# Dealing the weight conversion, the MLP work and two turnings of a fused HGRN2 + MLP kernel anew

## The chip, the cores and the metric

The kernel runs on one core of one Trainium2 chip. The metric is the device time of one launch in microseconds (us). The core has five engines that run side by side, each its own list of instructions in order, and wait for one another by semaphores: TensorE (PE) for matmuls, with its weight loads shown as PEld, VectorE (DVE), ScalarE (ACT), GpSimd (POOL), and SyncE (SP), which here only starts DMA transfers.

## The reference

```python
def _attn_ref(q, k, v, f_logit):          # each (4, 8, 768, 48)
    f = 1.0 / (1.0 + np.exp(-f_logit))
    state = np.zeros((B, H, D, D))
    for t in range(S):
        state = f[:, :, t, :, None] * state + np.einsum('bhd,bhe->bhde', k[:, :, t], v[:, :, t])
        y[:, :, t] = np.einsum('bhd,bhde->bhe', q[:, :, t], state)
    return y

x = attn_out.transpose(0, 2, 1, 3).reshape(B * S, H * D)      # 3072 tokens x 384
h = x @ w_in                                                  # 384 x 2048
g = h * (1.0 / (1.0 + np.exp(-1.702 * h)))
out = g @ w_out                                               # 2048 x 384
```

A gated linear recurrence over 768 steps in four batches of eight heads makes the tokens; an MLP with a quick GELU follows.

## The kernel before, in words

**Units.** The 3072 tokens are cut into 12 units of 256 tokens, three for each batch, numbered 0 to 11. For each unit the recurrence is computed in chunks of 64 tokens: `turn` (L325) brings f, q and k with tokens along the columns (for units 0 to 2 by matmuls, L339, from unit 3 on by a DVE transpose, L327); six levels of products within a chunk follow, each a set of score matmuls (L384), a masked evacuation from PSUM on DVE (L410, tile A), a product of A with v (L448, into y) and a promotion of q and k by the gates of that level (L436, L437 or L439 on DVE, with copies Kc and Qc on ACT, L423). `turn_k` (L498) transposes the keys for the states (matmul L505, copy kn L506); L523 multiplies them with v, L538 to L543 carry the states from chunk to chunk on DVE, and L563 adds the states' part to y. At last y goes through ACT (yT, L571) and six DMA transfers (L592, L597) into xT, the 384 x 256 input of the MLP.

**Parts.** `parts_of(n)` (L814) lists what a unit does as parts, each with a letter: W or V for a level or two levels, T for half of the key transposes, S for the states, B and K for beginning the next unit. Beginning the next unit means `begin_f` (turn f, apply the sigmoid, start the load of the f after next), `begin` (turn q, two small POOL copies of its last column, start the next load of q), `begin_k` and `begin_gates`. From unit 3 on the f and q of the next unit are begun together in one part of letter B.

**MLP work.** The MLP of finished units waits in a list `fill`, in items of a weight in columns: an item of the first product (tile h, three matmuls of 256 columns, L727, followed by the sigmoid on ACT, L732, and the product g on DVE, L733) weighs 768, one of the second (o, L755) 384. From unit 3's tokens on the second product is done with seven half-size products instead of eight (L704), from sums of weights (T, L622) and of g (L641 to L650). `merge` (L848) writes out a unit's parts and deals `columns` of this list between them: after each part comes a portion according to `share` of its letter (W 3, V 4, S 3, T, B and K 1). An item is only taken if the weights that it needs are ready.

**Weights.** The weights come as 64-bit floats, and the kernel itself makes 32-bit floats of them. They are 32 pieces of 128 x 384. A pair of pieces is fetched by one or two DMA transfers into a tile `bits`, of which there are three (L180), and each piece is then converted by one copy on ACT (L208) and five operations on DVE (L223, L219, L226, L227, L228). `convert` (L231) issues one of these DVE operations; `merge` deals 5 x `pieces` of them over its unit, before all MLP items that follow them. A pair that is done starts the fetch of another. Unit 0 has conversion work, but no MLP work yet.

**Order.** PE's order is that in which the program writes its instructions. The other engines follow the written order up to the end of unit 3 (`fill_order`, L90 and L907); behind it the framework's scheduler places their instructions. The last number of `merge`, `by`, is the part of the unit by which its conversion is to be done.

Of the kernel before, what the change touches and what calls it, by code (L numbers as in the profile page):

```python
# [23 lines left out]
def kernel(  # L24
# [34 lines left out]
    B, H, S, D = q.shape  # L59
    DM = H * D  # L60
# [16 lines left out]
    N_FILL = 3  # L77
# [153 lines left out]
    def convert():  # L231

        if state["begin"] < len(pairs) and len(todo) <= NOP:
            begin_pair(state["begin"])
            state["begin"] += 1
        if todo and todo[0]:
            todo.pop(0)()
        if todo and todo[0] is None:
            todo.pop(0)
            state["done"] += 2  # L240
            fetch_weights()
# [34 lines left out]
    def load_vl(n, l):  # L276

        if n >= NALL:
            return
        t = vls[n, l] = ld.tile([P, DM], F32, tag=f"vl{l}", name=f"vl_{n}_{l}")  # L280
        if n < N_TURN:
            pt = ps.tile([P, DM], F32, tag="mm", name=f"tv_{n}_{l}", bufs=4)
            for g in range(NG):
                nc.tensor.matmul(
                    pt[g * 64:(g + 1) * 64], lhsT=perm[:, l - 1, :] if l else ident[:, ::2], rhs=vns[n][:, g, :],
                    start=True, stop=True,
                )
            nc.scalar.copy(t, pt)
            return
        nc.sync.dma_start(out=t, in_=v_toks[n % 2].rearrange("(n two m) e -> two n m e", two=2, m=LEV[l])[0])  # L290
# [507 lines left out]
    def mlp_blocks(*blocks):  # L798

        hs, os = zip(*(mlp_block(n, r) for n, r in blocks))  # L800
        return sum(hs, []) + sum(os, [])


    def keep_up(times):

        if times:
            pt = ps.tile([P, NL * 64], F32, tag="mm", name=f"idle_{next(serial)}", bufs=4)
        for _ in range(times):
            nc.tensor.matmul(pt, lhsT=ident, rhs=masks.rearrange("p l t -> p (l t)"), start=True, stop=True)

    units = [attention(n) for n in range(NALL)]
    LAG = 18 * DM

    def parts_of(n):  # L814

        parts = list(units[n][1])
        _, inter = parts.pop()
        if n:
            kind, scores = parts[0]
            _, ahead = units[n - 1][1][-1]  # L820
            parts[0] = kind, lambda: (ahead(), scores())
        if n < N_TURN:

            def with_v(l):
                kind, fn = parts[l]
                return kind, lambda: (fn(), load_vl(n, l) if n == 0 or l else None, keep_up(2 * (n == 0 and l < 3)))
            parts[:NL] = [with_v(l) for l in range(NL)]
        if n + 1 < NALL:
            begin_f, begin, begin_k, begin_gates = units[n + 1][0]
            i = len(parts)  # L830
            if n + 1 < N_FILL:

                parts.append(("K", lambda: (begin_k(), begin_gates(), load_vl(n + 1, 0) if n + 1 < N_TURN else None)))
                parts.insert(i - 4, ("B", begin if n == 0 else lambda: None))
                parts.insert(i - 5, ("B", begin_f))
                if n:

                    kind, head = parts[0]
                    parts[0] = kind, lambda: (head(), begin())
            else:  # L840
                kind, states = parts.pop()
                parts += [("B", begin_k), (kind, lambda: (states(), begin_gates()))]
                parts.insert(i - 3, ("B", lambda: (begin_f(), begin())))
        else:
            parts.append(("W", inter))
        return parts

    def merge(n, fill, columns, share, pieces=0, hold=0, by=1.0, chores=()):  # L848

        parts = parts_of(n)
        total = sum(share(kind) for kind, _ in parts)
        converting = {"W": 3, "T": 3, "B": 1} if n < N_FILL - 1 else {"W": 3, "V": 4, "S": 3, "T": 1, "B": 1}
        total_ops = sum(converting.get(kind, 0) for kind, _ in parts)
        held = sum(share(kind) for kind, _ in parts[:hold])
        at = at_ops = done = ops = 0
        for kind, fn in parts:
            ready = state["done"]
            fn()  # L860
            for chore in chores[:2]:
                chore()
            chores = chores[2:]
            at += share(kind)
            at_ops += converting.get(kind, 0)
            n_ops = min(int(pieces * NOP * at_ops / (by * total_ops)), pieces * NOP) - ops
            ops += n_ops
            first, n_columns = done, max(0, columns * (at - held) / (total - held) - done)

            def some(end):  # L870
                nonlocal done
                while fill and done < end and fill[0][2] <= ready:
                    w, emit, _ = fill.pop(0)
                    emit()
                    done += w
            for i in range(n_ops):
                some(first + n_columns * i / n_ops)
                convert()
            some(first + n_columns)
# [4 lines left out]
    UNIT = NFF * NK * U + U // P * NFF * DM  # L884
# [12 lines left out]
        load_raw(1, j)  # L897
    load_vn(1)
    fill = []
    merge(0, fill, 0, steady, 8)  # L900
    fill += mlp_blocks((0, 0)) + mlp_blocks((0, 1))
    merge(1, fill, UNIT // 2 - LAG // 2, steady, 10, hold=1)
    fill += mlp_blocks((1, 0), (1, 1)) + mlp_blocks((0, 2), (1, 2))
    merge(2, fill, UNIT, steady, 8)
    fill += mlp_blocks((2, 0), (2, 1)) + mlp_blocks((2, 2), (0, 3)) + mlp_blocks((1, 3), (2, 3))
    merge(3, fill, 3 * UNIT // 2 - LAG // 2, steady, 6, by=0.7)
    fill_order.close()  # L907
    for n in range(3, NALL):
        fill += mlp_unit(n)
# [33 lines left out]
```

## Time and profile before

| | us |
|---|---|
| median of four runs | 657.4 (655.48 to 658.79) |
| the profiled execution | 657.54 |
| its span, first to last instruction | 655.5 |
| PE busy | 634.5 (97% of the span) |
| DVE busy | 444.9 (68%) |
| ACT busy | 229.8 (35%) |
| POOL busy | 54.7 (8%) |

The busy time of PE is the time in which at least one matmul is under way. Units 0 to 11 follow each other in the span: unit 0 ends at about 44 us, unit 1 at 86, unit 2 at 143, unit 3 at 211, and from there each takes some 49 us, up to the MLP of the last unit at the end. [...]

### The profile page before, as it was taken

What the parts mean: (1) busy time and instruction counts of PE and PEld (TensorE: products, weight loads), DVE (VectorE), ACT (ScalarE), POOL (GpSimd) and SP (SyncE); (2) the same over time, 40 slices, a digit from 0 to 9 for tenths busy, and PEclk for the clock granted to TensorE, in tenths of its full rate; (3) what the DMA queues carried; (4) which work ended last, traced back from release to release, by engine and by line L of the source; (5) the groups of instructions that cost most, each with busy time, mean ns of one, the idle gap of its engine ahead of it and who ended that gap; (6) DMA issues with size and microseconds to landing.
All of it is one profiled execution on the core that took longest, in us unless ns stands there. A gap on an engine that the chain in (4) does not pass through costs nothing.

```text
span 655.5 us, 20397 instructions
## 1 busy us (share of the span) xinstructions
PE 634.5 (97%) x8958; PEld 543.2 (83%) x8958; DVE 444.9 (68%) x802; ACT 229.8 (35%) x477; POOL 54.7 (8%) x116
## 2 busy tenths in 40 slices
PE   6969989999999999999999999999999999999997
PEld 5656667666678689989989989989989889989997
DVE  2997978788887657658658558558558557553571
ACT  4473443233224324324324324324324334222120
POOL 3020020020001002002002002002002002000000
PEclk9997999999999999999999999999999999999999
DMA  8887875394135544524514515605604202101000
GB/s 190 217 210 192 203 172 134 93 216 79 34 72 141 147 94 119 149 46 119 155 37 121 155 37 120 165 27 124 162 27 105 66 25 62 39 2 26 25 1 24
DMA packets 67554, 67.67 MB, mean 103 GB/s; under 512 B 30410, under 2 KB 61290, under 8 KB 67466
## 3 DMA queue, kind: packets, MB, share of 16 engines
q1 hardware_dynamic: 67466, 66.38, 40.5%
q8 instruction: 70, 1.15, 0.8%
q14 instruction: 18, 0.15, 0.1%
HBM read 56.92 MB, written 8.65 MB: 100 GB/s over the span
## 4 chain that ended last, share of the span: by engine, by line
PE 85%; DVE 8%; SPq 2%; DMA 2%; ACT 1%; issue 1%; DVEq 0%; ACTq 0%
PE h L727 37%; PE o_X L704 7%; PE o L755 7%; PE o_Y L704 7%; PE o_Z L704 7%; PE sc L384 5%; PE y L448 5%; PE o_W L704 4%; PE y L563 2%; PE sc L523 1%; PE tkn L505 1%; DMA bits<-in_moe_w_in_dram 1%; DVE X L439 1%; SPq L251 1%; DVE s L219 1%
## 5 line engine op out<-in xcount | busy, mean ns | idle before, releaser
L727 PE MATMUL h<-xT,w_in 128*128 128x256 f32 (+1 forms) x1152 | 261.7, 383 | 4.4 <-DMA xT<-yT 1.8
L727 PEld LDWEIGHTS h<-xT,w_in 128*128 128x128 f32 x1152 | 216.7, 191 | 38.9 <-issue 3.1
L733 DVE TENSOR_TENSOR g<-h,sg 128x256 f32<-128x256 f32 (+1 forms) x192 | 80.9, 423 | 100.4 <-ACT sg L732 98.0
L732 ACT ACTIVATE sg<-h 128x256 f32<-128x256 f32 (+1 forms) x192 | 73.4, 384 | 194.5 <-PE h L727 189.7
L423 ACT COPY Kc<-X 128x512 f32<-128x512 f32 x69 | 46.2, 669 | 118.1 <-DVE X L439 84.7
L755 PE MATMUL o<-w_out,g 128*128 128x384 f32 x192 | 66.1, 493 | 0.0
L439 DVE TENSOR_TENSOR X<-X,tot 128x1024 f32<-128x1024 f32 x45 | 55.1, 1225 | 15.3 <-PE sc L384 10.2
L755 PEld LDWEIGHTS o<-w_out,g 128*128 128x128 f32 x192 | 35.3, 190 | 22.9 <-issue 1.4
L704 PE MATMUL o_X<-w_out,g 128*128 128x192 f32 x288 | 51.9, 329 | 0.0
L704 PE MATMUL o_Y<-T,S 128*128 128x192 f32 x288 | 51.1, 331 | 0.1
L704 PEld LDWEIGHTS o_Y<-T,S 128*128 128x128 f32 x288 | 46.5, 190 | 2.6 <-DVE u L679 1.2
L704 PEld LDWEIGHTS o_X<-w_out,g 128*128 128x128 f32 x288 | 47.3, 190 | 0.9
L410 DVE TENSOR_TENSOR A<-sc,masks 128x512 f32<-128x512 f32 x72 | 46.8, 680 | 0.0
L448 PE MATMUL y<-A,vl 64*48 64x64 f32 x2304 | 41.6, 218 | 1.5 <-issue 1.4
L376 POOL TENSOR_TENSOR tot<-F 128x512 f32<-128x512 f32 x12 | 12.5, 1042 | 350.3 <-DVE st L540 350.3
L448 PEld LDWEIGHTS y<-A,vl 64*48 64x48 f32 x2304 | 36.5, 121 | 5.0 <-issue 4.7
L327 DVE STREAM_TRANSPOSE X<-raw 128x1024 f32<-128x1024 f32 x18 | 36.7, 2037 | 2.4 <-PE y L563 2.0
L571 ACT COPY yT<-y 48x512 f32<-48x512 f32 x48 | 27.9, 580 | 12.5 <-PE y L563 12.0
L384 PEld LDWEIGHTS sc<-X,Kc 48*64 48x64 f32 x1344 | 23.9, 134 | 8.3 <-issue 3.5
L384 PE MATMUL sc<-X,Kc 48*64 48x64 f32 x1344 | 28.1, 219 | 1.9 <-DVE A L410 1.2
L376 POOL TENSOR_TENSOR tot<-tot 128x256 f32<-128x256 f32 (+4 forms) x60 | 27.4, 458 | 4.7
L704 PE MATMUL o_Z<-w_out,g 128*128 128x192 f32 x144 | 26.6, 331 | 0.0
(93 smaller groups left out, 656.9 us busy)
## 6 DMA issues: line engine op xcount, KB each, us to landing
vl<-v_tok SPq DMA_DIRECT2D x60, 192.0 KB, 2.8
bits<-in_moe_w_out_dram SPq DMA_DIRECT2D x8, 768.0 KB, 10.2
bits<-in_moe_w_in_dram SPq DMA_DIRECT2D x8, 576.0 KB, 7.1
v_tok<-in_v_dram SPq DMA_DIRECT2D x10, 384.0 KB, 4.4
vn<-v_tok SPq DMA_DIRECT2D x10, 384.0 KB, 6.8
xT<-yT SPq DMA_DIRECT2D x24, 144.0 KB, 2.8
raw<-in_q_dram SPq DMA_DIRECT2D x18, 192.0 KB, 4.2
raw<-in_f_logit_dram SPq DMA_DIRECT2D x18, 192.0 KB, 4.9
```

The costliest lines, as they stand in the source:

```text
L327: nc.vector.transpose(out.rearrange("p (a i j) -> p a j i", a=NP, j=R), raw[:, j].rearrange("p a (j d) -> p (a j) d", j=R)[:, :, :32],)
L376: nc.gpsimd.tensor_tensor(tn, t2[:, :, 0], t2[:, :, 1], ALU.mult)
L384: nc.tensor.matmul(out[g * HS:(g + 1) * HS, h, a, :], lhsT=lhs(h, a * U + g * G), rhs=rhs(h, a * U + g * G), start=True, stop=True,)
L410: nc.vector.tensor_tensor(A[:, :, c:c + w].rearrange("p h (x t) -> p h x t", t=64), t["sc"][:, :, c:c + w].rearrange("p h (x t) -> p h x t ...
L423: nc.scalar.copy(c.rearrange("p (n m) -> p n m", m=m), X[:, j, :NA].rearrange("p (n two m) -> p n two m", two=2, m=m)[:, :, hf, :],)
L439: nc.vector.tensor_tensor(qk, qk, by, ALU.mult)
L448: nc.tensor.matmul(dst(h, g, a), lhsT=vls[n, u][g * 64:(g + 1) * 64, (2 * a + h) * D:(2 * a + h + 1) * D], rhs=A(h, g, a), start=(start an ...
L704: nc.tensor.matmul(t[bank], lhsT=lhs(f), rhs=rhs(f), start=(new and f == 0), stop=(f == HF - 1), skip_group_check=True,)
L727: nc.tensor.matmul(ph, lhsT=w_in[:, c, ff * P:(ff + 1) * P], rhs=xTs[n][:, c, :], start=(c == 0), stop=(c == NK - 1))
L732: nc.scalar.activation(sg, ph, AF.Sigmoid, scale=1.702)
L733: nc.vector.tensor_tensor(g[ff // FG][:, ff % FG, :], ph, sg, ALU.mult)
L755: nc.tensor.matmul(t["po"], lhsT=g[ff // FG][:, ff % FG, tt * P:(tt + 1) * P], rhs=w_out[:, ff, :], start=(ff == ffs[0]), stop=(ff == ffs[ ...
```

## The change

Three things change, all in how work is dealt.

1. The 32 weight pieces are dealt over units 0 to 3 as 6, 10, 9 and 7 instead of 8, 10, 8 and 6.
2. By the end of unit 1, 3 x 384 = 1152 columns less of MLP work have been issued, and in unit 2 1152 more, so that from the end of unit 2 on the amount done is as before.
3. When the next unit is unit 5 or a later one (in `parts_of` n is above 3), f and q are begun in two parts instead of one: f behind the third pair of levels, as before, and q one part later, behind the first half of the key transposes. The unit so has one more part of letter B, and the shares of its parts add up to 20 instead of 19.

```diff
             else:
                 kind, states = parts.pop()
                 parts += [("B", begin_k), (kind, lambda: (states(), begin_gates()))]
-                parts.insert(i - 3, ("B", lambda: (begin_f(), begin())))
+                if n > N_FILL:
+                    parts.insert(i - 3, ("B", begin_f))
+                    parts.insert(i - 1, ("B", begin))
+                else:
+                    parts.insert(i - 3, ("B", lambda: (begin_f(), begin())))
...
     fill = []
-    merge(0, fill, 0, steady, 8)
+    merge(0, fill, 0, steady, 6)
     fill += mlp_blocks((0, 0)) + mlp_blocks((0, 1))
-    merge(1, fill, UNIT // 2 - LAG // 2, steady, 10, hold=1)
+    merge(1, fill, UNIT // 2 - LAG // 2 - 3 * DM, steady, 10, hold=1)
     fill += mlp_blocks((1, 0), (1, 1)) + mlp_blocks((0, 2), (1, 2))
-    merge(2, fill, UNIT, steady, 8)
+    merge(2, fill, UNIT + 3 * DM, steady, 9)
     fill += mlp_blocks((2, 0), (2, 1)) + mlp_blocks((2, 2), (0, 3)) + mlp_blocks((1, 3), (2, 3))
-    merge(3, fill, 3 * UNIT // 2 - LAG // 2, steady, 6, by=0.7)
+    merge(3, fill, 3 * UNIT // 2 - LAG // 2, steady, 7, by=0.7)
```

## The prediction

> **What bounds the kernel now.** I read the page first, then busy time by stretch, then the timeline inside the stretches that were not full. On the page TensorE (PE) is busy 97% of the span, so only the remaining 21 us, and stretches whose clock is low, can be won without removing matmuls. The stretches show where they lie (columns: stretch; its length; busy us and instruction count of PE, weight loads, VectorE = DVE, ScalarE = ACT, GpSimd; granted PE clock; DMA share; GB/s):
>
> ```profile
> 14.00:44.00 30.00, 25.48 (x623) 17.45 (x622) 29.72 (x67) 14.70 (x28) 1.54 (x6) 1.00 0.86 212
> 44.00:57.00 13.00, 10.68 (x148) 7.83 (x152) 8.03 (x18) 6.74 (x12) 4.19 (x8) 0.74 0.81 194
> 57.00:86.00 29.00, 29.00 (x560) 20.74 (x561) 28.02 (x68) 14.14 (x30) 0.42 (x1) 1.00 0.83 219
> 86.00:95.00 9.00, 7.25 (x113) 4.66 (x114) 7.79 (x15) 4.64 (x8) 3.21 (x6) 1.00 0.65 135
> 95.00:127.00 32.00, 32.00 (x366) 24.34 (x367) 22.20 (x50) 9.31 (x21) 0.00 (x0) 1.00 0.46 117
> 127.00:160.00 33.00, 29.33 (x346) 20.73 (x347) 29.39 (x52) 13.18 (x27) 3.76 (x8) 1.00 0.66 147
> 160.00:258.00 98.00, 98.00 (x1241) 77.70 (x1234) 70.83 (x119) 31.03 (x66) 7.00 (x13) 1.00 0.38 98
> 258.00:566.00 308.00, 307.92 (x4695) 283.09 (x4695) 204.67 (x325) 110.02 (x227) 29.41 (x52) 1.00 0.37 94
> ```
>
> Unit 0 (14 to 44 us) has no MLP work to fill PE, and DVE is full there: 29.72 of 30.00. In unit 1 (57 to 86) both engines are nearly full. From 160 us on PE has no gap: what DVE does there is hidden, up to the idle time that it has. The end of unit 0, where PE waits for DVE and ACT, in the timeline (start, duration, engine, line; in brackets the idle time before and its releaser):
>
> ```profile
> 34.08 0.68 DVE L436 TENSOR_TENSOR X<-X,tot 128x512 f32<-128x512 f32 x1
> 34.91 1.07 PE L505 MATMUL tkn<-ident,X 128*128 128x128 f32 x8 [1.07 <-DVE X L436]
> 37.21 1.00 ACT L208 ACTIVATE a<-bits 128x384 f32<-128x384 f32 x2 [0.91 <-DMA bits<-in_moe_w_in_dram]
> 38.11 0.56 ACT L506 COPY kn<-tkn 128x512 f32<-128x512 f32 x1
> 38.73 0.68 PE L523 MATMUL sc<-vn,kn 64*64 64x48 f32 x32 [1.50 <-ACT kn L506]
> 40.31 1.02 DVE L219 SCALAR_TENSOR_TENSOR s<-bits,a 128x384 int32<-128x384 int32 x2
> 41.25 0.35 DVE L538 COPY st<-sc 128x192 f32<-128x192 f32 x1
> ```
>
> **Part 1: two pieces fewer in unit 0.** Two pieces are ten DVE operations. In pairs the rows read 0.62 (L223), 1.02 (L219), 0.62 (L226), 1.02 (L227), 1.02 us (L228): 4.30 us. Not all of it is on the path. The first level scores start at 21.07, 24.43, 28.04 and 31.90, and between them PE is full (gaps of 0.72 and 0.17 only, and the first of them waits for ACT, which waits for weight bits), so DVE running ahead wins 0.17 there at most. The gain lies after 31.9. I walk the new order with the old durations. L436 of the last level, now behind four pending conversion operations instead of six, can start when its score ends, at about 32.7 instead of 34.08; the key transposes (L505) follow at 33.7, not 34.91. In the new ACT order the two L208 copies stand before the first key copy, and none is left between the two key copies: they end at 36.1 and 36.7 (before: 36.29 and 38.67). The second half of L523 ends at about 37.4, not 39.4. The DVE chain from the last evacuation to the first state copy (L538) holds 11 conversion operations instead of 14: from 34.6 on, 0.5 + 0.62 + 1.02 + 1.02 + 0.62 + 1.02 = 4.8 us, so L538 at 39.4 against 41.25. **-1.85 us.** The bounds are the PE gaps that could go at most (4.5 us in the stretch) and no gain at all, if the arrival of weight bits (ACT waited 1.50 and 0.91 us for them) holds the new order too.
>
> **Part 2: 1152 columns fewer by the end of unit 1.** In the new order that is two hidden tiles (h_0_6, h_0_7), each six matmul records. Twenty-four such records take 5.42 us in the row at 94.87, two tiles 2.6 us with overlap. Do they shorten unit 1? Only if PE sets its end. The states (L540) start at 82.67, though their matmuls (L523) ended at 80.07: DVE was still converting. Ten pieces are converted in unit 1 in both kernels, and only one product g (0.42 us) leaves the queue ahead of the states. **-0.4**; PE then idles some 2.6 us before the last y. That work goes into the hand-over to unit 2:
>
> ```profile
> 86.61 5.43 PE L755 MATMUL o<-w_out,g 128*128 128x384 f32 x16
> 94.87 5.42 PE L727 MATMUL h<-xT,w_in 128*128 128x256 f32 x24 [1.75 <-DMA xT<-yT]
> ```
>
> From the end of y (86.0) to that h are 8.9 us, the way of y through ACT and DMA into xT. PE has 7.1 us of work for them; with 2.6 more it has 9.7. The wait of 1.75 goes, and 0.8 us is now PE's own. **+0.8**, so the move by itself returns about 0.4 and wins nothing: the 2.6 us that it takes from unit 1 were hidden behind DVE.
>
> **Part 3: one piece more in unit 2, one more in unit 3.** Each is five DVE operations, 2.15 us, with one L208 copy of 0.5 us on ACT and its share of a weight fetch on the SP queue. Cover: from 95 to 127 DVE idles 9.8 us, from 160 to 258 27 us, while PE has no gap. The fetches come later by a pair; their stretches have a DMA share of 0.46 and 0.38. Without cover the two would cost 4.3. The open place is 127 to 160, where DVE works 29.39 of 33 and PE loses 3.67:
>
> ```profile
> 126.85 2.05 DVE L327 STREAM_TRANSPOSE F<-raw 128x1024 f32<-128x1024 f32 x1
> 128.74 2.02 DVE L327 STREAM_TRANSPOSE X<-raw 128x1024 f32<-128x1024 f32 x1
> 130.85 2.86 PE L727 MATMUL h<-xT,w_in 128*128 128x256 f32 x12 [1.33 <-ACT kn L506]
> 153.33 2.96 PE L727 MATMUL h<-xT,w_in 128*128 128x256 f32 x12 [0.85 <-DVE sum L793]
> ```
>
> In the new order the two turnings stand one g earlier, so that g waits behind them, its PSUM buffer comes free later, and the stall at 130.85 can grow by some 0.9. Against that, between the turnings and the first g of unit 2's MLP stand 18 conversion operations instead of 16 (+0.95) but neither of the two L622 subtractions (-1.82). I take **0**, from -1.5 to +2.
>
> **Part 4: f and q apart.** This concerns the turnings of units 5 to 11. DVE is not in written order there, the scheduler places it, and the listing of both kernels has the same DVE order in these units: F, one or two L650, then q, as in the trace:
>
> ```profile
> 305.82 2.05 DVE L327 STREAM_TRANSPOSE F<-raw 128x1024 f32<-128x1024 f32 x1 [0.83 <-DMA vl<-v_tok]
> 307.71 1.29 DVE L650 TENSOR_TENSOR g<-g,S 128x512 f32<-128x512 f32 x2
> 309.38 2.06 DVE L327 STREAM_TRANSPOSE X<-raw 128x1024 f32<-128x1024 f32 x1 [0.38 <-PE y L563]
> ```
>
> They are apart already: q must wait for the y of the unit before. With q go its two POOL copies (0.65 and 0.41 us) and four loads of raw q on the SP queue; in the listing these trade places with two output stores and two vl loads, and raw q is turned a unit, 48 us, later. What does change is the spread: one more part of share 1 makes 20 shares of 19, so a V part gets 4608 of the 23040 columns instead of 4851, 0.4 us of PE less before the next score. The next score's keys are ready at 315.86, PE reaches it at 318.86: slack 3 us. PE is busy 307.92 of 308.00. **0**; from -2 (o_Y groups at 2.87 instead of 2.60) to +1.
>
> **The clock, rule against row.** From 49 to 56 us the granted clock was half, after PE had been busy 0.77, 0.47, 0.30 and 0.30 in four slices of a microsecond:
>
> ```profile
> 48.00:49.00 1.00, 0.30 (x18) 0.15 (x10) 1.00 (x3) 1.00 (x3) 0.45 (x2) 1.00 0.15 30
> 49.00:50.00 1.00, 0.30 (x13) 0.30 (x16) 1.00 (x3) 0.28 (x2) 0.40 (x1) 0.64 0.20 57
> 50.00:51.00 1.00, 1.00 (x31) 0.86 (x25) 1.00 (x2) 0.71 (x1) 0.00 (x0) 0.50 0.62 134
> ```
>
> The longest single gap there was 1.40 us, and the first twelve h records took 4.76 us instead of some 2.7: 2.1 us. The Trainium skill ("TensorE: Matmul & The Clock Gate", on HAM oscillation) asks for gaps under about 3.4 us, and adds that the window runs free of the kernel. By the gap rule the 2.6 us of new idle time in unit 1 cost nothing; by the row a thin stretch is enough, and a drop there would cost as much as here: 7 us at half clock, 3.4 us of work. The measurement decides that it can happen. For the likeliest case I leave the old drop where it is and add none; the range holds both.
>
> **Sum.** -1.85 - 0.4 + 0.8 + 0 + 0 = -1.45 us on the profiled execution, 657.54 (span 655.5 and 2.0 around it): 656.1. Its time is 0.1 above the median of 657.4, so I forecast 655.9: -0.2%, a small gain, inside what a measurement of this kernel can tell (0.5%, 3.3 us; the four runs spread over 3.3).
>
> **Rivals.** *The relief is larger:* with DVE ahead, PE is denser around 46 to 50 us and the clock drop goes (-2.1), and the stalls of 0.85 and 0.51 us near 155 close with the L622 moved back (-1.4): 655.9 - 3.5 = 652.4. For it: DVE is full in unit 0. Against: the chain y, ACT, xT around 46 us is the same in both kernels. *A new clock drop makes it slower:* unit 1 leaves PE idle 2.6 us before the last y at about 82; if that halves the clock for 7 us, the hand-over, now full of PE work, pays all 3.4 us: 659.3; with the stall at 130.85 grown as bounded, 661. It decides from a drop of about 3 us on, which loses the 1.5 won. *The turnings matter:* if a score's chain were late by 0.4 us once a unit, seven units would cost 2.8: 658.7; the slack of 3 us speaks against. *Nothing happens:* weight bits hold unit 0 as before: 657.8.
>
> **How the numbers follow.** Likeliest case 0.45 (own range 654.3 to 657), larger relief 0.25, clock drop 0.15, turnings 0.05, nothing 0.10. Over 0.5% faster needs under 654.1: most of the relief case and a little of the first, 0.30. Over 0.5% slower needs over 660.7: part of the drop case and mis-sized edges, 0.12. Same 0.58. The range leaves out one in ten on each side: 652 to 660.5.
>
> **What would show it.** After: L538 of unit 0 near 39.4; no wait for xT in front of the first h of unit 1's tokens, which starts near 93.4; PE idle between 75 and 83; PE full from 160 us on, and units 48.5 to 48.8 us apart. Wrong would be: a gap in front of a score after 258 us, a half clock elsewhere, or a stall of more than 3 us between 125 and 160.

## The result

The changed kernel takes 654.07 us (median of 38 runs, 651.58 to 661.53) against 657.78 (57 runs, 655.42 to 661.44) for the kernel before on the same chip: ratio 0.9953, 95% interval 0.9942 to 0.9965. It was measured a second time beside other variants (experiment 10): 655.4 against 657.13, ratio 0.9970 (0.9945 to 0.9996). The ratios are taken from the fast runs alone (one of the 38, at 661.53, was slow) and are not the quotient of the medians, which is 0.9944. The forecast was 655.9, with -0.2%; measured was, by the two ratios, -0.3% and -0.5%. The profiled execution took 654.37 us, its span is 652.2 (before: 655.5), PE is busy for 632.5 us of it.

Busy time by stretch of the changed kernel (stretch; its length; busy us and instruction count of PE, weight loads, DVE, ACT, POOL; granted PE clock; DMA share; GB/s):

```profile
14.00:44.00 30.00, 27.29 (x692) 19.07 (x683) 27.64 (x61) 16.06 (x31) 4.57 (x9) 1.00 0.92 218
44.00:57.00 13.00, 11.09 (x177) 7.46 (x175) 10.14 (x22) 7.16 (x14) 2.24 (x6) 0.87 0.75 160
57.00:86.00 29.00, 27.79 (x517) 20.07 (x518) 27.88 (x66) 15.67 (x33) 3.63 (x6) 1.00 0.91 234
86.00:95.00 9.00, 9.00 (x94) 6.12 (x93) 6.75 (x15) 2.08 (x5) 0.00 (x0) 1.00 0.49 94
95.00:127.00 32.00, 30.23 (x361) 22.56 (x359) 25.60 (x51) 10.56 (x24) 0.41 (x2) 1.00 0.44 117
127.00:160.00 33.00, 29.57 (x440) 22.04 (x441) 28.04 (x53) 12.05 (x26) 3.40 (x7) 1.00 0.72 167
258.00:566.00 308.00, 308.00 (x4590) 284.45 (x4583) 203.53 (x325) 109.39 (x229) 28.02 (x48) 1.00 0.37 94
```

DVE is no longer full in unit 0 (27.64 of 30, was 29.72), PE is fuller there (27.29, was 25.48), the granted clock in the second row is 0.87 (was 0.74), and the hand-over to unit 2 (86 to 95) has no gap. PE loses 1.21 us in unit 1 (57 to 86), where it lost nothing before. The 1.77 us that it loses from 95 to 127 belong to a stall that stood in the next row before; the two rows together lose 5.20, and lost 3.67.

The end of unit 0 in the timeline (start, duration, engine, line; in brackets the idle time before and its releaser):

```profile
32.68 0.69 DVE L436 TENSOR_TENSOR X<-X,tot 128x512 f32<-128x512 f32 x1
32.73 0.69 PE L384 MATMUL sc<-X,Kc 48*64 48x64 f32 x32
34.60 1.10 PE L505 MATMUL tkn<-ident,X 128*128 128x128 f32 x8
34.70 0.55 DVE L219 SCALAR_TENSOR_TENSOR s<-bits,a 128x384 int32<-128x384 int32 x1
36.66 1.17 PE L523 MATMUL sc<-vn,kn 64*64 64x48 f32 x64 [0.38 <-ACT kn L506]
39.05 0.35 DVE L538 COPY st<-sc 128x192 f32<-128x192 f32 x1
```

L538 comes at 39.05 (was 41.25), although this execution began late: its third score stands at 22.14 (was 21.07; this differs from run to run). From the third score to L538 are 16.91 us, where there were 20.18: unit 0 is 3.3 us shorter.

The hand-over to unit 2 and the boundary from unit 2 to unit 3 in the timeline of the changed kernel:

```profile
85.28 3.39 PE L755 MATMUL o<-w_out,g 128*128 128x384 f32 x10
89.68 2.20 PE L755 MATMUL o<-w_out,g 128*128 128x384 f32 x6
91.87 3.48 PE L727 MATMUL h<-xT,w_in 128*128 128x256 f32 x15
...
122.56 2.05 DVE L327 STREAM_TRANSPOSE F<-raw 128x1024 f32<-128x1024 f32 x1
124.44 2.03 DVE L327 STREAM_TRANSPOSE X<-raw 128x1024 f32<-128x1024 f32 x1
127.43 4.15 PE L727 MATMUL h<-xT,w_in 128*128 128x256 f32 x18 [2.21 <-ACT kn L506]
150.90 5.45 PE L727 MATMUL h<-xT,w_in 128*128 128x256 f32 x24 [1.67 <-DVE sum L793]
```

The wait of 1.75 us for xT is gone. The stall for kn has grown from 1.33 to 2.21 us, and one of 1.67 for the sum L793 stands where 0.85 (for L793) and 0.51 (for a g) stood. Why PE waits longer for kn, the copy of the transposed keys, stands in ACT's order. Before:

```profile
130.22 0.58 ACT L506 COPY kn<-tkn 128x512 f32<-128x512 f32 x1
131.42 1.06 ACT L208 ACTIVATE a<-bits 128x384 f32<-128x384 f32 x2
```

After:

```profile
125.66 0.98 ACT L208 ACTIVATE a<-bits 128x384 f32<-128x384 f32 x2
126.80 0.57 ACT L506 COPY kn<-tkn 128x512 f32<-128x512 f32 x1
```

With the new deal of pieces two conversion copies (0.98 us) stand on ACT ahead of the first key copy. From the third score on, with the time lost to half clock taken out (3.4 us before, 1.7 after), the difference splits so:

| from, to | before | after | difference |
|---|---|---|---|
| third score to L538 (unit 0) | 20.18 | 16.91 | -3.3 |
| to the first score of unit 2 (unit 1) | 41.3 | 41.2 | -0.1 |
| to the first score of unit 3 (unit 2) | 57.2 | 58.8 | +1.6 |
| to the end | 512.3 | 511.4 | -0.9 |
| sum | 631.0 | 628.4 | -2.7 (rounded) |

Read the single rows with care: experiments 3 and 4 below, one program in effect, differ by 1.0 us in the row of unit 1 and by 1.6 in the last, but by 0.2 in the sum. The 1.6 us of unit 2 are mostly work: PE has twelve h matmuls more to do there and two o matmuls fewer, 2.0 us by the rates of the rows shown (5.42 us for 24 and 5.43 for 16), and stands still for 3.4 us instead of 3.7.

The rest of the 3.3 us between the two spans is no merit of the change: 1.7 us less half clock, against 1.1 us of later start.

The last row holds a gain in the later units, which are now 48.5 us apart (were 48.5 to 48.8; the first distance, 48.4, is the same in both). Two stretches of timeline show it. Before, in unit 7:

```profile
361.42 2.76 PE L704 MATMUL o_Z<-T,g 128*128 128x192 f32 x16
362.68 1.24 DVE L439 TENSOR_TENSOR X<-X,tot 128x1024 f32<-128x1024 f32 x1 [0.17 <-ACT Qc L423]
363.82 0.35 DVE L679 TENSOR_TENSOR u<-p,o_Y 128x192 f32<-128x192 f32 x1
364.22 2.57 PEld L704 LDWEIGHTS o_Y<-T,S 128*128 128x128 f32 x16 [0.33 <-DVE u L679]
364.22 2.87 PE L704 MATMUL o_Y<-T,S 128*128 128x192 f32 x16
```

After, in the same unit:

```profile
359.04 2.76 PE L704 MATMUL o_Z<-T,g 128*128 128x192 f32 x16
360.74 0.35 DVE L679 TENSOR_TENSOR u<-p,o_Y 128x192 f32<-128x192 f32 x1
361.64 1.46 PE L704 MATMUL o_Y<-T,S 128*128 128x192 f32 x8
363.03 0.69 PE L384 MATMUL sc<-Qc,Kc 48*64 48x64 f32 x32
365.02 1.24 PE L704 MATMUL o_Y<-T,S 128*128 128x192 f32 x6
```

The second o_Y group goes on in the PSUM tile that L679 reads, so it can't start before L679 is through. Before, L679 stood on DVE behind the promotion L439 of the score just done, and PE lost 0.33 us. After, L679 is done 0.5 us ahead of the group, and the score cuts the group in two. In the list of waits of the weight loads from 258 to 566 us the kernel before has 1.2 us of this in four waits, the changed kernel none.

### The profile page after: what moved, and what is told of

The parts are those of the page before. It is cut to its first block, busy times and chain, and to the rows that moved or that the text cites. A ratio compares the mean times of both kernels' runs of the same rounds, so it can differ in the third digit from the quotient of the medians.

```text
span 652.2 us, 20388 instructions
## 1 busy us (share of the span) xinstructions
PE 632.5 (97%) x8958; PEld 543.6 (83%) x8958; DVE 445.0 (68%) x802; ACT 229.2 (35%) x477; POOL 55.0 (8%) x116
## 3 DMA queue, kind: packets, MB, share of 16 engines
q8 instruction: 70, 1.15, 0.8%
## 4 chain that ended last, share of the span: by engine, by line
PE 86%; DVE 6%; DMA 3%; SPq 2%; ACT 1%; issue 1%; DVEq 0%; ACTq 0%
PE h L727 37%; PE o_X L704 8%; PE o_Y L704 7%; PE o L755 7%; PE o_Z L704 7%; PE sc L384 5%; PE y L448 5%; PE o_W L704 4%; DMA bits<-in_moe_w_in_dram 2%; PE y L563 2%; PE sc L523 1%; PE tkn L505 1%; DVE s L219 1%; SPq L180 1%; SPq L251 1%
## 5 line engine op out<-in xcount | busy, mean ns | idle before, releaser
L439 DVE TENSOR_TENSOR X<-X,tot 128x1024 f32<-128x1024 f32 x45 | 55.2, 1227 | 33.9 <-PE sc L384 29.1
L704 PE MATMUL o_X<-w_out,g 128*128 128x192 f32 x288 | 53.8, 331 | 0.0
L704 PE MATMUL o_Z<-T,g 128*128 128x192 f32 x144 | 24.9, 326 | 0.0
(93 smaller groups left out, 660.5 us busy)
```

The lines of the kernel that those rows point to most:

```text
L439: nc.vector.tensor_tensor(qk, qk, by, ALU.mult)
L704: nc.tensor.matmul(t[bank], lhsT=lhs(f), rhs=rhs(f), start=(new and f == 0), stop=(f == HF - 1), skip_group_check=True,)
```

## The experiments

Each was run in five rounds beside the kernel before: 1 to 4 on one chip, 5 to 8 on a second, 9 to 11 on a third, 12 on a fourth. Times are best compared on one chip; from chip to chip go by the ratios. "Rest" in the table is the span less the start of the third score and less the time lost to half clock after it (the sum of one minus the granted clock, from rows of one us). It is a rough measure: part of a loss can be hidden, so it is good to about 1 us. The last column is the time from the first L563 behind 190 us to the last.

| run | median, us | ratio (95%) | span | third score | clock loss | rest | L563 to L563 |
|---|---|---|---|---|---|---|---|
| before (profiled) | | | 655.5 | 21.07 | 3.4 | 631.0 | 384.2 |
| after (profiled) | 654.07 | 0.9953 (0.9942 to 0.9965) | 652.2 | 22.14 | 1.7 | 628.4 | 383.0 |
| 1 pieces alone | 654.70 | 0.9975 (0.9956 to 0.9993) | 653.8 | 21.19 | 3.4 | 629.2 | 384.2 |
| 2 columns alone | 655.71 | 0.9993 (0.9978 to 1.0008) | 653.3 | 21.24 | 0 | 632.1 | 383.0 |
| 3 turnings alone | 655.98 | 0.9998 (0.9983 to 1.0013) | 655.4 | 21.25 | 3.4 | 630.7 | 384.2 |
| 4 empty part | 655.03 | 0.9989 (0.9971 to 1.0006) | 653.2 | 21.00 | 1.7 | 630.5 | 384.2 |
| 5 apart from unit 3 on | 653.65 | 0.9971 (0.9948 to 0.9995) | 650.3 | 21.16 | 3.4 | 625.7 | 382.9 |
| 6 PE kept busier | 655.54 | 0.9999 (0.9975 to 1.0023) | 652.2 | 21.17 | 1.7 | 629.3 | 382.9 |
| 7 after without the columns | 653.56 | 0.9965 (0.9941 to 0.9988) | 650.2 | 21.26 | 0 | 628.9 | 384.2 |
| 8 four pieces in unit 0 | 656.44 | 1.0010 (0.9989 to 1.0031) | 652.8 | 21.08 | 0 | 631.7 | 382.9 |
| 9 as 5, without the columns | 653.91 | 0.9966 (0.9941 to 0.9991) | 654.4 | 23.64 | 5.1 | 625.6 | 384.2 |
| 10 after again | 655.40 | 0.9970 (0.9945 to 0.9996) | 656.8 | 21.49 | 6.8 | 628.5 | 383.0 |
| 11 as 5, again | 652.38 | 0.9917 (0.9889 to 0.9946) | 650.7 | 21.89 | 3.4 | 625.4 | 382.9 |
| 12 as 9, one tile later | 653.14 | 0.9946 (0.9925 to 0.9966) | 653.9 | 21.50 | 1.7 | 630.7 | 383.0 |

### Each part alone

**1. The pieces.** The kernel before with:

```diff
-    merge(0, fill, 0, steady, 8)
+    merge(0, fill, 0, steady, 6)
...
-    merge(2, fill, UNIT, steady, 8)
+    merge(2, fill, UNIT, steady, 9)
...
-    merge(3, fill, 3 * UNIT // 2 - LAG // 2, steady, 6, by=0.7)
+    merge(3, fill, 3 * UNIT // 2 - LAG // 2, steady, 7, by=0.7)
```

> The new deal of pieces alone (6, 10, 9, 7), the rest as before. My theory (DVE relief in unit 0 is the gain): the first state copy of unit 0 (L538) at 39 to 40 us instead of 41.25, the wait for xT before the first h of unit 1's tokens stays, and 1.5 to 2.5 us are won at the end: ratio 0.9962 to 0.9977. Rival (the columns carry the gain by filling the wait for xT): under 0.5 us, ratio above 0.999. Rival (weight bits hold unit 0): L538 stays at 41 us, no gain.

Faster, 0.9975, and the only part whose interval alone leaves 1 out. Its timeline:

```profile
38.10 0.36 DVE L538 COPY st<-sc 128x192 f32<-128x192 f32 x1
...
89.85 7.11 PE L727 MATMUL h<-xT,w_in 128*128 128x256 f32 x24 [2.73 <-DMA xT<-yT]
128.39 4.54 PE L727 MATMUL h<-xT,w_in 128*128 128x256 f32 x12 [2.20 <-ACT kn L506]
152.49 5.45 PE L727 MATMUL h<-xT,w_in 128*128 128x256 f32 x24 [1.54 <-DVE sum L793]
```

From the third score to L538 are 16.91 us, as in the changed kernel: the whole gain of unit 0 is the pieces'. But unit 2 takes 1.1 us more: in it PE waits for xT for 2.73 us instead of 1.75, and for kn for 2.20 instead of 1.33. These stalls are the pieces' too, not the columns', and so is the one of 1.54 for L793. (Unit 1 reads 0.6 us more, which is within the error of a row.) Of 3.3 us some 1.8 remain.

**2. The columns.** The kernel before with:

```diff
-    merge(1, fill, UNIT // 2 - LAG // 2, steady, 10, hold=1)
+    merge(1, fill, UNIT // 2 - LAG // 2 - 3 * DM, steady, 10, hold=1)
...
-    merge(2, fill, UNIT, steady, 8)
+    merge(2, fill, UNIT + 3 * DM, steady, 8)
```

> The 1152 columns alone, pieces and turnings as before. My theory: unit 1 is ended by DVE, so the moved work was hidden there: the wait for xT goes, but the first h of unit 1's tokens starts no earlier, and the time is the same, +0.4 us (ratio 0.999 to 1.002). Rival (the filled wait of 1.75 us is won): ratio 0.997 to 0.998.

Not told from no change (0.9993). The wait for xT at the hand-over is gone here too, and the stall for kn is 1.33 us, as before. But its last L563 stands 383.0 us behind the first, not 384.2. The row of tile y from 190 to 640 us (duration in ns least/median/most, starts of the first and the last instruction):

```profile
L563 PE MATMUL y<-X,st x576: 163/216/253, 208.7 to 591.7; 48*48 48x64 f32 x174, 48*48 48x1 f32 x18
```

**3. The turnings**, that is the change in `parts_of` alone.

```diff
-                parts.insert(i - 3, ("B", lambda: (begin_f(), begin())))
+                if n > N_FILL:
+                    parts.insert(i - 3, ("B", begin_f))
+                    parts.insert(i - 1, ("B", begin))
+                else:
+                    parts.insert(i - 3, ("B", lambda: (begin_f(), begin())))
```

> The turnings of units 5 to 11 in two parts, pieces and columns as before. By the trace after: a unit takes 48.5 instead of 48.7 us, because the second group of o_Y no longer waits for L679: 1.2 to 1.6 us won over seven units, ratio 0.9975 to 0.9985. By the step of the prediction (nothing): ratio 1.000.

No change (0.9998). Its units have the times of the kernel before, 48.4 to 48.8 us, and the wait for L679 is there as before. The same row of tile y, and the list of waits of the weight loads from 258 to 566 us (total, times, longest):

```profile
L563 PE MATMUL y<-X,st x576: 162/216/253, 210.9 to 595.1; 48*48 48x64 f32 x174, 48*48 48x1 f32 x18
```

```profile
PEld sc L384 <- issue: 3.6, 13, 0.3
PEld y L563 <- issue: 1.6, 7, 0.2
PEld y L448 <- issue: 1.4, 6, 0.2
PEld o_Y L704 <- DVE u L679: 1.2, 4, 0.3
```

**4. f and q together, and an empty part.** The kernel before with the one more share of letter B and nothing in it:

```diff
                 parts.insert(i - 3, ("B", lambda: (begin_f(), begin())))
+                if n > N_FILL:
+                    parts.insert(i - 1, ("B", lambda: None))
```

> f and q begun together as before, but an empty part of letter B where q would be begun, so that the MLP work is spread over 20 shares. If the spread makes the gain in the steady units: the same as with the turnings apart, units of 48.5 us, ratio 0.9975 to 0.9985. If the place of q's turning makes it: units of 48.7 us as before, ratio 1.000.

By the traces the instructions of this kernel stand in the same order as those of experiment 3 (on PE compared without the small products within a unit, whose order differs between executions of one program): "apart" changes nothing at all in units 5 to 11, since the scheduler places q's turning by its own waits. The two runs (0.9998 and 0.9989) are two measurements of one program, and so the 1.0 us between their medians is scatter. I had at first put the gain of the steady units to the extra share. These two runs rule that out: with the share, and without the columns, the L563 stand 384.2 us apart.

**7. The changed kernel without the columns.**

```diff
-    merge(1, fill, UNIT // 2 - LAG // 2 - 3 * DM, steady, 10, hold=1)
+    merge(1, fill, UNIT // 2 - LAG // 2, steady, 10, hold=1)
...
-    merge(2, fill, UNIT + 3 * DM, steady, 9)
+    merge(2, fill, UNIT, steady, 9)
```

> The kernel after with the 1152 columns put back: pieces and turnings alone. My theory (the move of columns wins nothing): the wait for xT before the first h of unit 1's tokens is back, 1.3 us or more, and the time is that of the kernel after or up to 0.6 us less (ratio 0.994 to 0.9955). Rival (it belongs with the pieces, which bring the wait for xT forward): 1 to 2 us slower than the kernel after, ratio 0.997 to 0.9985.

0.9965, level with the changed kernel on other chips (0.9953, 0.9970) and between the two expectations. The wait for xT is back (1.74 us), the L563 are 384.2 us apart, and the rest is 628.9 against 628.4: what the columns win behind unit 2 (511.4 us to the end with them, 512.1 without) they lose in unit 2 (58.8 us with them, 57.8 without).

### What the columns do to the later units

Over the kernels up to experiment 11 the L563 are 382.9 to 383.0 us apart in each kernel with the moved columns and 384.2 in each without them, whatever else is changed. The timelines show why they reach so far. Behind the first L563 of unit 3, kernels with the moved columns begin with six h records, a hidden tile, that the others have done before it; and at the last L563 the changed kernel has done 4 of the 16 o_X matmuls of the stretch, the kernel before 12. So the MLP work is one hidden tile (weight 768) behind in units 4 to 11, and it comes up for that at the end: 61.6 us behind the last L563, not 60.3. These 1.3 us at the end are the hidden tile that was not done ahead of the first L563 of unit 3, so they are moved, not lost; the 1.3 us between the L563 are won. So "from the end of unit 2 on as before", as I had described the columns, holds for the numbers dealt, not for what is issued: items are taken whole.

**12. One tile later, without the columns.** On the kernel of experiment 9, unit 3 deals 768 columns less:

```diff
-    merge(3, fill, 3 * UNIT // 2 - LAG // 2, steady, 7, by=0.7)
+    merge(3, fill, 3 * UNIT // 2 - LAG // 2 - 2 * DM, steady, 7, by=0.7)
```

> Pieces 6, 10, 9, 7, f and q apart for units 3 to 11, no columns moved, and unit 3 deals 768 columns (one hidden tile) less. Earlier runs fall in two groups by the time from the first L563 after 190 us to the last L563 of the span: 382.9 to 383.0 us in every kernel with the moved columns, 384.2 to 384.3 in every kernel without them, and only the second group shows the wait of the second o_Y group for L679 (1.2 us, 4 times). My theory now: the moved columns do this, not by where they were put, but because they leave the MLP work one hidden tile behind from unit 3 on, so that a score cuts the second o_Y group. It expects 382.9 to 383.0 here, no such wait, a tail 1.3 us longer, and about 1 us less in all than in the run without this lag. Rival (something else that the moved columns do): 384.2 to 384.3, and the wait stays. The median should be 651.5 to 654.5, ratio 0.990 to 0.996.

The time between the L563 is 383.0, 61.6 us follow, and the wait for L679 is gone. The row of tile y and the list of waits as above:

```profile
L563 PE MATMUL y<-X,st x576: 162/216/253, 209.3 to 592.3; 48*48 48x64 f32 x174, 48*48 48x1 f32 x18
```

```profile
PEld sc L384 <- issue: 3.6, 13, 0.3
PEld y L448 <- issue: 1.4, 6, 0.2
PEld y L563 <- issue: 1.4, 6, 0.2
```

So the place of the MLP work against the scores does it, not the columns as such. That it makes the whole faster by the 1 us expected isn't shown: 0.9946 against 0.9966 is within the intervals, and the rest of the profiled execution (630.7) holds a stall of 2.96 us, long before unit 3 and the edit (timeline of this run):

```profile
44.70 0.24 PE L563 MATMUL y<-X,ident 48*48 48x1 f32 x2 [2.96 <-issue]
```

### The boundaries and the clock

**5, 11. f and q apart from unit 3 on**, in the changed kernel, twice:

```diff
-                if n > N_FILL:
+                if n > 1:
```

> The kernel after, with f and q begun apart from unit 3 on instead of unit 5 on. Up to the end of unit 3 DVE follows the written order, so here the two transposes really part. My theory (two transposes in a row keep the g behind them waiting): the stall of PE of 2.21 us at about 127 falls under 1.2 us, and 1 to 1.5 us are won against the kernel after (about 0.993 of the kernel before). Rival (the stall is ACT's sigmoid of F in front of the key copy, which stays): 2 us stall as before, no gain.

> The changed kernel with f and q begun apart for the turnings of units 3 and 4 too, a second time. Theory: the stall of 1.3 to 2.2 us for kn near 127 goes (0.52 in the first look) and a wait for st of some 2 us stands at 136, so it is at most 1 us faster than the changed kernel beside it. Rival (the stretch that sets the end of unit 2 does get shorter, as the clean sum of the first look had it): 2 to 3 us faster than the changed kernel beside it, about 0.991.

In units 2 and 3 the written order holds on DVE, and there it does matter. In the timeline of experiment 11:

```profile
122.99 1.56 PE L727 MATMUL h<-xT,w_in 128*128 128x256 f32 x6 [0.52 <-ACT kn L506]
136.00 0.32 PE L563 MATMUL y<-X,st 48*48 48x64 f32 x4 [2.19 <-DVE st L543]
```

The stall for kn falls from 2.21 to 0.52 and the one for L793 goes (1.67), as the turnings no longer stand in one piece on DVE (F at 119.00 and q at 124.95; in the changed kernel at 122.56 and 124.44). With F earlier the key copy kn stands on ACT ahead of the conversion copies again (122.36 and 122.83), and PE has twelve h matmuls to do ahead of the wait instead of six. 1.7 us come back as a wait for the states, which stand on DVE behind the turnings of q and k (124.95 and 129.26). The rest is 625.4 and 625.7, 3 us under that of the changed kernel; these stalls make 1.7 of it, and what makes the remainder isn't shown.

Beside the changed kernel on the same chip (experiment 10) experiment 11 is 3.0 us faster, and the runs don't overlap (six from 651.76 to 652.87, twelve from 653.27 to 659.91): the rival's number, not my theory's. Experiment 5 had no changed kernel on its chip, and its 0.9971 is no better than the ratios of that kernel elsewhere; but its timed runs lost more to half clock (4.6 us in the median, taken as the span times one minus the granted clock, against 2.0 and 3.6 for the changed kernel). So a gain is likely, and its size is open.

**9. The same without the columns**: the edits of 5 and 7 together.

> The same without the moved columns: pieces 6, 10, 9, 7 and the turnings of units 3 to 11 begun apart. Theory (the columns win nothing; their wait for xT near 89 is paid by a shorter boundary between units 2 and 3): within 1 us of the run with the columns. Rival (the columns hide the wait for xT of 1.7 us at no other price): 1.5 to 2 us slower than the run with the columns.

0.9966, and the rest is 625.6, level with that of experiment 11 (625.4). The clocked median, though, is 1.5 us above that of experiment 11 on the same chip (653.91 and 652.38), as the rival had it. The timed runs of 9 lost 5.2 us to half clock in the median, those of 11 only 3.3, so whether the columns win anything here stays open.

**6. PE kept busier at the thin stretch.** In the changed kernel, two matmuls of the kind that unit 0 already has there, into a tile that nobody reads, ahead of the second level of units 1 and 2 and two behind it:

```diff
             parts[:NL] = [with_v(l) for l in range(NL)]
+            if n:
+                kind_1, level_1 = parts[1]
+                parts[1] = kind_1, lambda: (keep_up(2), level_1(), keep_up(2))
```

> The kernel after, with two matmuls of no use (128 x 384) ahead of the second score of unit 1 and two behind its v matmuls, in the waits around 46 to 50 us. If thin stretches of PE make the half clock there: no half clock between 44 and 57 us, which is worth 1.5 to 3 us in a run that had it, and the median 1 to 2 us lower than that of the kernel after (ratio 0.992 to 0.994). If the half clock falls by chance wherever the window lies: it still shows in some place, and the time is that of the kernel after or up to 1 us more.

The half clock near 48 us was gone, but this execution had one from 125 to 129, behind a stall of 2.20 us. That it is gone shows little: seven of the other profiles have none between 40 and 57 us either. No gain: 0.9999, and 655.54 beside the 653.56 of experiment 7 on the same chip.

**8. Four pieces in unit 0**: 4, 11, 10 and 7, in the changed kernel.

```diff
-    merge(0, fill, 0, steady, 6)
+    merge(0, fill, 0, steady, 4)
...
-    merge(1, fill, UNIT // 2 - LAG // 2 - 3 * DM, steady, 10, hold=1)
+    merge(1, fill, UNIT // 2 - LAG // 2 - 3 * DM, steady, 11, hold=1)
...
-    merge(2, fill, UNIT + 3 * DM, steady, 9)
+    merge(2, fill, UNIT + 3 * DM, steady, 10)
```

> The kernel after with pieces dealt 4, 11, 10, 7. If DVE was still the bound in unit 0: from the second score to the first state copy (L538) 18 to 19 us instead of 20.9, and 1.5 us more won. If PE is the bound now: that stretch shortens by less than 0.7 us, and the piece more in units 1 and 2 costs as much or more (unit 1 is ended by DVE: about 2 us), ratio 0.996 to 0.999.

Unit 0 is shorter again, 15.44 us from the third score to L538: DVE still bounded a part of it (from the second score 18.8 us, as the first case had it). But it doesn't pay: 1.0010 instead of 1.5 us more won, slower than the changed kernel. In its timeline PE then stands still for 2.13 us (no releaser shown), 2.05 (xT), 0.95 (states of unit 1) and 1.81 (g). What is taken from unit 0 has to be done in units 1 and 2; in unit 1 DVE is already full in the changed kernel (27.88 of 29.00 us from 57 to 86).

**10. The changed kernel again.**

> The changed kernel once more, beside two variants. My theory (2 us from two pieces fewer in unit 0, under 1 us from the spread over 20 shares, nothing from the columns, and a half clock that falls in another place each time): ratio 0.9945 to 0.9970, about 653.5. The rival that the gain of the first comparison was mostly a luckier place of the half clock: 0.997 to 1.000.

0.9970, where the two expectations meet. Its profiled execution, 658.91 us, is 4.5 longer than the first of the same program. Three stretches of half clock account for it: 6.8 us lost against 1.7, with a start 0.65 us earlier.

## Why the prediction was right, step by step

**The whole.** 655.9 was forecast with a range of 652 to 660.5; 654.07 came, inside the range, below the likeliest case's own 654.3 by 0.2. By the traces, clock and start aside, the change is worth -2.7 us, where the sum said -1.45. Sorted by place, the terms of the sum read -1.85 (unit 0), -0.4 (unit 1), +0.8 and +0.9 (unit 2) and -0.87 (behind it, the set-off of part 3); measured are -3.3, -0.1, +1.6 and -0.9. The last number agrees by luck: the set-off did not come, and a gain that was not foreseen did.

**Part 1** (-1.85): the mechanism was right and the size off. L538 came 3.3 us earlier behind the third score, or up to 4.0: the four profiles with the old deal have 20.2 to 21.0 us there, the nine with the new one 16.9 to 17.1. (The scores that the step lists, at 21.07 to 31.90, are those of levels three to six.) Two terms of the walk were mis-sized. L436 was let wait for the last score's end; it doesn't need it and starts beside it (32.68 against 32.73), so the last evacuation was through at 34.70, 12.56 us behind the third score where the walk had 13.53: 1.0 us. And the eleven operations from there to L538 took 4.35 us instead of 4.8. The bound of "no gain, because the weight bits arrive late" did not come true.

**Part 2** (+0.4 together): right for what it looked at. In unit 1 -0.1 (-0.4 predicted). The wait for xT went, and the first h of unit 1's tokens started at 91.87 without one (93.4 predicted; unit 0 was shorter than in the walk). The +0.8 of the hand-over fits unit 2: 58.8 us in the changed kernel, 57.8 in experiment 7. "Wins nothing" holds as far as it was tested: 0.9993 alone, no difference between 7 and the changed kernel, and for 9 and 11 none in the rest (the clocked medians are 1.5 us apart). What the step left out is that a deal in whole tiles shifts all later work by one tile; that is worth -1.3 us between the L563 of units 3 and 11, and about as much is lost before.

**Part 3** (0, from -1.5 to +2): this is the step with the wrong centre, in both of its terms.

The stall for kn grew "by some 0.9", as written (1.33 to 2.21), but not for the reason given, so the number was luck. The step let a g wait behind the turnings and its PSUM buffer come free late. In the traces PE waits for the key copy on ACT, and what now stands ahead of that copy are the two conversion copies L208, 0.98 us. Two experiments tell the reasons apart: experiment 2 has four g between the turnings of q and k, as the changed kernel has (three before), but the old pieces, and its stall is 1.33; experiment 1 has three g and the new pieces, and its stall is 2.20.

The set-off did not come: L793 is awaited for 1.67 us, where 0.85 and 0.51 had been. The step counted the two L622 subtractions as gone from in front. In the kernel before they stand behind the L793 that PE waits for (started at 152.73), and only ahead of the g of the stall of 0.51:

```profile
154.60 1.82 DVE L622 TENSOR_TENSOR T<-w_out 128x768 f32<-128x768 f32 x2
```

So that stall went, and the wait for L793 could not get shorter. From the first score of unit 3 to the L793 that PE waits for are 9.54 us before, 10.20 with the pieces alone, 8.85 with the columns alone and 9.53 with both: the added conversion delays it by 0.7 (the step had +0.95). In the changed kernel PE gets to it 0.8 us sooner, with less work in front.

**Part 4** (0): right, and for the reason given. The order on DVE was already that, and experiments 3 and 4 are one program in effect. The bound of -2 named the right place, o_Y groups at 2.87 us, but the wrong cause: they sped up by the columns, and the extra share did nothing that these runs show.

**The clock** (left as is): what half clock took was 1.7 us in the changed kernel's first profile and 6.8 in its second, 3.4 before; the traces give no sign that the change did this (see below). The rival "larger relief" was right that more would be won, but neither of its reasons came: the stalls near 155 grew (1.36 to 1.67 us), and the clock drop near 48 did not go. The rival "new clock drop" did not come in the median: in experiment 10 the timed runs of the changed kernel lost 3.6 us to the clock, those of the kernel before 3.3.

**Signs named ahead.** L538 near 39.4: 39.05. No wait for xT: none. PE idle in unit 1, some 2.6 us: 1.2. PE full from 160 on, units 48.5 to 48.8 apart: 48.5. No stall over 3 us between 125 and 160: 2.21. Half clock elsewhere, named as a sign of being wrong: none in the first profile up to 650 us, but at 84 and 131 us in the second.

## What to carry to other kernels

Taking work from an engine that is full in one stage wins time there, but the work has to be done in another stage, which may be as full: with the pieces alone some 1.8 of 3.3 us won in unit 0 remained, and with two pieces more moved nothing was left. Work has companions on other engines: the stall for kn grew by a conversion copy on ACT, not by the DVE operations that had been counted. Ask what stands in front of the very instruction that is awaited. Where work is dealt in whole items, compare where each item stands in all later stages too: one tile's shift in units 1 and 2 shortened six later units by 0.05 to 0.3 us each, 1.3 in all. Before a gain is put to a part, group all runs by each part: I first gave the steady gain to the turnings, and the row of one tile in all the profiles showed that it went with the columns.

## What the runs showed of the hardware

**Half clock comes in pieces of 3.4 us and by chance.** In eleven of the fourteen profiles the granted clock fell to half, between the third score and 160 us, in stretches of about 3.4 or 6.8 us, each 3.4 us costing 1.7 us of PE work, at places that differ between executions of one program: the changed kernel had one stretch at 47 us in one profile, and three from 43, 84 and 131 us in the other. Here is one in experiment 1, behind the wait of 2.73 us (same columns as above):

```profile
90.00:91.00 1.00, 1.00 (x5) 0.88 (x6) 0.00 (x0) 0.00 (x0) 0.00 (x0) 1.00 1.22 187
91.00:92.00 1.00, 1.00 (x4) 0.82 (x3) 0.00 (x0) 0.33 (x1) 0.00 (x0) 0.50 0.04 4
92.00:93.00 1.00, 1.00 (x4) 0.82 (x3) 0.69 (x2) 0.05 (x1) 0.00 (x0) 0.50 0.00 0
93.00:94.00 1.00, 1.00 (x4) 0.73 (x4) 0.00 (x0) 0.00 (x0) 0.00 (x0) 0.50 0.87 190
94.00:95.00 1.00, 1.00 (x5) 0.86 (x4) 0.29 (x1) 0.38 (x1) 0.00 (x0) 0.80 0.90 292
```

PE is full in these rows; the clock falls a microsecond after the stall is over. The matmuls confirm it: the 24 h records that begin at 89.85 take 7.11 us, where 24 took 5.42 before. Between the third score and 160 us the profiles hold 16 such drops and 20 stalls of PE of 1.8 to 3.0 us. Twelve of the stalls have a drop that begins around their end or within 2 us of it; of 17 stalls of 1.3 to 1.75 us one has. Three drops stand behind shorter stalls (0.46 to 0.81). If the stalls bring the drops, a stall of 2 us costs, beside itself, some 1 us more on average (an estimate: 12 in 20 times 1.7; more where the drop lasts 6.8), and one of 1.5 hardly anything. It is no certainty: the change made one such stall, for kn, out of a shorter one (1.33 to 2.2 us), and in experiments 1, 6 and 10 a drop stands behind it, in the changed kernel's first profile and in experiment 7 none.

The Trainium skill ("TensorE: Matmul & The Clock Gate", what's actually happening) gives the window as 3413 ns, running freely; the length agrees. Its advice to leave no gaps over about 3 us (same page, "Why this matters for your kernels") would let all 20 of these stalls pass; if they bring the drops, it is not strict enough for this kernel.

Drops are a large part of why one program's times spread over 10 us: of the 38 timed runs of the changed kernel the three fastest lost 0.65 us each to the clock (span times one minus the granted clock), the three slowest 3.3, 5.3 and 8.6.

**PE can stand still in the middle of a row of ready matmuls.** In four of the fourteen profiles (the changed kernel twice, experiments 8 and 12) PE paused for 0.70, 2.41, 2.13 and 2.96 us among the last L563 of unit 0, with no releaser shown. Experiment 12's row is above. The traces hold a likely cause. The profile lists a queue q8 of kind "instruction" with 70 packets and 1.15 MB, which is 64 bytes for each of the 17,916 matmuls and weight loads, so it looks like PE's own list (an estimate). All four pauses are in front of the same matmul, and the fifth q8 packet of the span, 16,384 bytes, lands 1.3 to 1.6 us before that matmul starts (at 40.79, 41.82, 40.42 and 43.32 us; the matmul at 42.11, 43.43, 41.77 and 44.70). In the other ten profiles the packet lands 1.4 to 5.7 us ahead of it. With the new pieces the lead is 1.3 to 1.8 us, with the old ones 2.1 to 5.7: a shorter unit 0 brings PE closer to the arrival of its instructions. No run moved these packets, so this is argued from the times and not shown by an experiment.

**How early unit 0 gets going varies.** The third score starts between 21.0 and 23.6 us, and at different times in two executions of one program: 22.14 and 21.49 in the changed kernel. It moves the whole span. The latest, in experiment 9, had half clock from 14 to 21 us.
